# The causal triangle of an attention kernel: zeroed by GpSimd after the exponential, instead of added by matmuls before it

## The chip, the cores and the metric

The kernel runs on one core of a Trainium2 chip. The core has five engines that run their own instruction queues in order and meet through semaphores: TensorE (PE, matmuls into PSUM), VectorE (DVE), ScalarE (ACT), GpSimd (POOL) and SyncE (SP, which issues DMAs). The metric is the device time of one execution in microseconds; before the change it was 471.11 us, the median of three runs (469.35 to 471.49).

## The reference

Four blocks act on x, 2048 tokens by 512 channels in bfloat16: A, B, A, B, each added to its input. A is attention with 32 heads of 16 channels, in four segments of 512 tokens, causal within a segment, plus a memory that earlier segments fill. B is a linear attention with softmax features. The change touches A's causal mask above all.

```
# A, for each segment s
logits = einsum('bhqd,bhkd->bhqk', qs, ks) * scale + mask   # mask: -1e9 where key > query
p      = softmax(logits)
a_dot  = einsum('bhqk,bhkd->bhqd', p, vs)
pq, pk = phi(qs), phi(ks)                                   # phi(t) = t+1 if t > 0 else exp(t)
o      = g * (pq @ M) / (pq @ z + 1e-6) + (1 - g) * a_dot
M, z   = M + pk^T @ vs, z + sum(pk)
# then x = x + concat(o) @ wo;  before each block x is layer-normalised
```

## The kernel before

Tokens stand in 16 tiles of 128; a segment is four tiles. The whole of x stays in SBUF (`X`). For each tile `ln` takes mean and variance on DVE (L580, L581), the inverse root on GpSimd in two steps (L588 adds epsilon, L590 raises to the power -0.5), and the norm (x - mean) * rstd on DVE (L601). The result is transposed by a DMA, or by TensorE with `tpe` (L371) where `PE_T` names the tile.

`a_proj` makes keys and queries, transposed, for a segment. `kmask` (L642) copies the keys four times, each copy multiplied by a 0/1 column (`m4`) so that only one head of four is left (tile KM); `phi` (L632) makes the memory's features with an exponential on ACT and, on DVE, two clamps (L638, L639) and a sum (L640). All of these go from SBUF to SBUF.

`a_att` (L795) is called for two query tiles at a time (i0 = 0 and i0 = 2 of a segment). For each of the four head groups it makes score tiles S in PSUM with products that use 64 of TensorE's 128 rows each, two at a time side by side. There are three kinds of score tile: full ones below the diagonal (exponential into PT, 128 x 1024), two tiles of the query pair's own first key tile (`Sf`, exponential into PF, 896 columns) and one of the second key tile (`Sd`, into PE, 768 columns). Sf and Sd contain diagonal blocks of 64 x 64. On these, before the change, a further pair of products adds the triangle: the stationary `two64` (two identities side by side) times the moving `tri`, which holds -1e9 above the diagonal. ACT then takes the exponential of the whole tile, and the PV products use it with the values VT and their swapped copy VS (a DMA, "vsw").

```
# L828 (Sf) and L837 (Sd), the triangle's products at the end of each
(S.t[:, hf*512+64:hf*512+448].rearrange(...)[:, :, 0:64], two(hf), tri(hf, 2), False, True) for hf in range(2)
(S.t[:, hf*512:hf*512+384].rearrange(...)[:, :, 0:128],   two(hf), tri(hf, 4), False, True) for hf in range(2)
```

With 2 layers, 4 segments, 2 pairs of query tiles and 4 head groups there are 64 head-group passes, so 128 tiles PF and 64 tiles PE. PF lives in three buffers and PE in two (`N_PF`, `N_PE`); a buffer is opened by the score product and free again after the PV products. PSUM has four double tiles `D`, which score tiles, PV sums, projections and transposes share.

`out_proj` adds the output product to x; `b_keys` and `b_query` are block B. A few products use all 128 rows: the transposes of `tpe` (4 matmuls each), the sum of two halves in `o_T` (8 matmuls each, six times), the fold of B's feature weights in `fold_weights` (4 each, eight times), the product for the gates and the warm-up.

The order of the work is not decided in the code. `Graph.place` unpacks a table, `ORDER`: a position for every operation, the engine for each that may run on several, and a buffer for every tile. Each engine's queue follows these positions. `emit` then adds the semaphore waits that the data need; a wait is left out only between two operations of TensorE, so a GpSimd step that uses what an earlier GpSimd step wrote waits for it as well. Operations marked `port=True` are those that go from SBUF to SBUF.

Of the kernel before, what the change touches and what calls it, by code (L numbers as in the profile page):

```python
# [10 lines left out]
ALU = mybir.AluOpType  # L11
AX = mybir.AxisListType
BF16 = mybir.dt.bfloat16
F32 = mybir.dt.float32

S_TOK = 2048
D = 512
# [280 lines left out]
class Kernel:  # L298
# [72 lines left out]
    def tpe(self, out_ap, src, reads, writes, opens=(), label="", ev=None):  # L371

        ps = self.T(self.pD, "gen")
        pb = lambda: ps.t[:, :].bitcast(BF16)[:, 0:512]

        def fn(e):
            for k in range(4):
                ins = e.transpose(pb()[:, k * 128:(k + 1) * 128], src()[:, k * 128:(k + 1) * 128], self.ident[:])  # L378
            return ins
        self.g.op({"pe": (240.0, fn)}, list(reads) + [self.R("ident")], [ps], opens=opens, label=label + "p")  # L380
        if ev:
            self.evac(ev[0], lambda: ev[1](pb()), 512, [ps], writes, label=label + "e")
        else:
            self.evac(out_ap, lambda: pb().rearrange("p (a b) -> p a b", a=4), 512, [ps], writes, label=label + "e", fast=True)
# [11 lines left out]
    def alloc(self):  # L396
# [9 lines left out]
        self.two64 = sb("two64", [128, 2, 64], BF16)  # L406
# [43 lines left out]
    def setup(self):  # L450
# [43 lines left out]
        for g in range(NG):  # L494
            for hf in range(2):
# [16 lines left out]
        v(lambda e: e.tensor_tensor(self.two64[:], self.ident[:, 0:64][:, None, :].to_broadcast([128, 2, 64]),  # L512
                                    self.ident[:, 64:128][:, None, :].to_broadcast([128, 2, 64]), ALU.add), 120, [R("ident")], [R("two64")])
        tw = self.T(self.p1, "fold")
        v(lambda e: e.memset(tw.t[:, 0:128], -1e9), 150, [], [tw], eng=P)
        v(lambda e: e.affine_select(tw.t[:, 0:128], tw.t[:, 0:128], [[-1, 128]], ALU.is_gt, 0.0, base=0, channel_multiplier=1), 250, [tw], [tw], eng=P)
# [8 lines left out]
        self.mm(lambda: [(pb.t[:, 0:H], self.onesb[:], self.beta_sb[:], True, True)], [H], [R("beta0"), R("onesb")], [pb], label="beta")  # L525
# [22 lines left out]
    def fold_weights(self):  # L548
# [12 lines left out]
        for k in ("k", "q"):  # L561
# [7 lines left out]
            for dt in range(4):  # L569
                ps = self.T(self.pD, "gen")  # L570
                self.mm(lambda ps=ps, dt=dt, W=W: [(ps.t[:, g * 128:(g + 1) * 128], W.t[:, g, dt * 128:(dt + 1) * 128],
                                                    Wbd.t[:, g * 128:(g + 1) * 128], True, True) for g in range(NG)],
                        [128] * 4, [W[dt], Wbd], [ps], label="fold")
                self.evac(lambda k=k, dt=dt: self.WB[k][:, dt, :], lambda ps=ps: ps.t[:, 0:512], 512, [ps], [R("WB", k, dt)], label="folde")


    def ln(self, t, xT, flex=False, pe=False, root="pool"):
# [22 lines left out]
        else:  # L600
          v(lambda e: e.tensor_scalar(xn.t[:], self.X[:, t, :], self.mv[:, t, 0:1], self.rstd[:, t:t + 1],  # L601
                                    op0=ALU.subtract, op1=ALU.mult), 300,
          [R("X", t), R("mv", t), R("rstd", t)], [xn], label="xn", port=True)
# [28 lines left out]
    def phi(self, dst, src, e_, keys, c0, n):  # L632
# [5 lines left out]
        v(lambda e: e.tensor_scalar(cut(dst), cut(src), 0.0, None, op0=ALU.max), 68 + n / 3.84, S, D, label="phmax", port=True)  # L638
        v(lambda e: e.tensor_scalar(cut(e_), cut(e_), 1.0, None, op0=ALU.min), 68 + n / 3.84, E, E, label="phmin", port=True)  # L639
        v(lambda e: e.tensor_tensor(cut(dst), cut(dst), cut(e_), ALU.add), 68 + n / 1.92, D + E, D, label="phadd", port=True)  # L640

    def kmask(self, KM, KT, keys, c0, n, act):  # L642

        for sl in range(4):
            out = lambda sl=sl: KM.t[:, c0 // 128:(c0 + n) // 128, sl % 2, :, 64 * (sl // 2):64 * (sl // 2) + 64]
            src = lambda: KT.t[:, c0:c0 + n].rearrange("p (j h k) -> p j h k", h=2, k=64)
            ch = {"dve": (129 + n / 3.84, lambda e, sl=sl, out=out: e.tensor_scalar(out(), src(), self.m4[:, sl:sl + 1], None, op0=ALU.mult))}
            if act:
# [3 lines left out]
    def warm(self):  # L652
# [12 lines left out]
        for k in range(N_WARM):  # L665
            unit(128, 512, 1)
            if k == N_WARM // 2:
                for rows, n, m in ((64, 51, 12), (64, 64, 8), (64, 256, 4), (128, 34, 8)):
                    unit(rows, n, m)

    def a_proj(self, L, s):
# [66 lines left out]
        if s < 3:  # L738
            for hp in range(2):
# [10 lines left out]
                else:  # L750
# [3 lines left out]
                       [R("MS32", hp), R("GAm")], [R("MSb", s, hp)], label="Mmask")  # L754
# [523 lines left out]
```

## Time and profile before

| | |
|---|---|
| median of three runs | 471.11 us |
| span of the profiled execution | 465.9 us |
| instructions | 25071 |
| granted TensorE clock, mean | 0.999 |
| DVE instructions | 801 |
| GpSimd instructions | 139 |
| first to last triangle product, first layer | 16.5 to 181.3 us |
| first to last triangle product, second layer | 239.8 to 398.0 us |

The span runs from the first to the last instruction of the profiled execution and is shorter than the time of a run, which also has the start and the end of the program. Lines are named L and a number, as in the listing above. A busy share of TensorE counts overlapping matmuls once; a matmul's duration is longer than the interval to the next one, because they are pipelined. In rows of the trace "x4" means four instructions drawn together.

### The profile page before, as it was taken

To read this page: it belongs to the slowest core of one execution; us is meant where nothing else is said; L and a number is where in the kernel's file an instruction comes from. 1 tells how busy PE (TensorE), PEld (TensorE's weight loads), DVE (VectorE), ACT (ScalarE), POOL (GpSimd) and SP (SyncE) were. 2 spreads that over 40 slices of the span, in tenths; PEclk is the share of its full clock that TensorE was granted. 3 is DMA by queue.
4 is the path that set the end of the run, shared out by engine and by line. 5 is a ranking of instruction groups with operands and counts; after the bars stand their busy time and mean duration, and the time that the engine had idled before them with its cause. 6 is when DMAs were issued, how large, how long until landed. Compare 5 with 4: busy or idle time off the path is not lost.

```text
span 465.9 us, 25071 instructions
## 1 busy us (share of the span) xinstructions
PE 448.2 (96%) x11591; PEld 296.7 (64%) x11591; DVE 418.9 (90%) x801; ACT 424.3 (91%) x550; POOL 53.3 (11%) x139
## 2 busy tenths in 40 slices
PE   9999999999999999999999999999999999999886
PEld 4467656767767676655556777676677677666553
DVE  6999999999879988988999999999999787998991
ACT  4899999999999998589999999999999999686984
POOL 1401131001101101100320041010020020110000
PEclk9999999999999999999999999999999999999999
DMA  8363673403743031000143443441206104100247
GB/s 258 80 150 77 94 147 65 75 13 53 95 83 50 4 56 37 14 3 14 31 87 61 72 82 61 73 87 33 25 16 106 26 16 61 38 13 3 48 82 216
DMA packets 89386, 30.34 MB, mean 65 GB/s; under 512 B 75954, under 2 KB 89282, under 8 KB 89282
## 3 DMA queue, kind: packets, MB, share of 16 engines
q1 hardware_dynamic: 88450, 28.20, 32.5%
q8 instruction: 91, 1.49, 1.3%
q10 hardware_dynamic: 800, 0.52, 0.4%
q14 instruction: 13, 0.11, 0.1%
q0 software_dynamic: 32, 0.02, 0.0%
HBM read 6.31 MB, written 2.10 MB: 18 GB/s over the span
## 4 chain that ended last, share of the span: by engine, by line
PE 67%; ACT 26%; DVE 4%; issue 2%; POOL 1%; DVEq 0%
PE D L341 42%; PE D L326 23%; ACT p L351 12%; ACT pF L351 8%; ACT pE L351 4%; PE D L662 2%; DVE p L1091 1%; ACT pS L351 1%; PE D L378 1%; DVE p L360 1%; ACT X L359 1%; POOL rstd L590 1%; ACT p L359 0%; DVE p L601 0%; DVE p L1097 0%
## 5 line engine op out<-in xcount | busy, mean ns | idle before, releaser
L351 ACT ACTIVATE p<-D 128x1024 bf16<-128x1024 f32 (+1 forms) x224 | 222.0, 1026 | 13.2 <-PE D L341 10.0
L351 ACT ACTIVATE pF<-D 128x896 bf16<-128x896 f32 x128 | 116.1, 934 | 3.1 <-PE D L326 2.2
L326 PE MATMUL D<-pK,pQ 64*128 64x256 bf16 (+3 forms) x1536 | 114.8, 243 | 4.2 <-ACT pF L351 1.0
L326 PEld LDWEIGHTS D<-pK,pQ 64*128 64x128 bf16 x1536 | 55.1, 94 | 40.8 <-ACT pF L351 6.5
L326 PE MATMUL D<-pV,pF 64*128 64x34 bf16 x1024 | 76.4, 176 | 0.5 <-ACT pE L351 0.5
L326 PE MATMUL D<-pW,pF 64*128 64x34 bf16 x1024 | 74.1, 176 | 0.0
L326 PEld LDWEIGHTS D<-pV,pF 64*128 64x128 bf16 x1024 | 56.7, 93 | 3.7 <-issue 0.8
L588 POOL TENSOR_SCALAR rstd<-mv 128x1 f32<-128x1 f32 x60 | 15.2, 259 | 352.9 <-DVE mv L581 352.9
L326 PE MATMUL D<-pV,p 64*128 64x34 bf16 x1024 | 53.4, 176 | 0.6 <-issue 0.4
L326 PEld LDWEIGHTS D<-pW,pF 64*128 64x128 bf16 x1024 | 53.4, 93 | 1.0
L351 ACT ACTIVATE pE<-D 128x768 bf16<-128x768 f32 x64 | 52.4, 828 | 1.3 <-PE D L326 1.0
L326 PE MATMUL D<-pW,p 64*128 64x34 bf16 x1024 | 52.4, 176 | 0.0
L326 PEld LDWEIGHTS D<-pV,p 64*128 64x128 bf16 x1024 | 47.5, 93 | 3.2 <-issue 0.5
L326 PEld LDWEIGHTS D<-pW,p 64*128 64x128 bf16 x1024 | 46.0, 93 | 1.6
L326 PE MATMUL D<-tri,two 64*128 64x128 bf16 (+1 forms) x384 | 46.1, 234 | 0.0
L326 PE MATMUL D<-pV,pE 64*128 64x34 bf16 x512 | 45.1, 175 | 0.0
L580 DVE BATCH_NORM_STATS2 stats<-X 128x6 f32<-128x512 bf16 x64 | 42.7, 682 | 1.9 <-DMA X<-in_A_x_dram 1.5
L326 PE MATMUL D<-pW,pE 64*128 64x34 bf16 x512 | 43.4, 175 | 0.0
L972 DVE TENSOR_REDUCE pS<-p 128x64 f32<-128x1024 bf16 (+1 forms) x36 | 38.8, 1089 | 1.4 <-ACT p L351 1.4
L341 PE MATMUL D<-pX,WA_q 64*128 64x512 bf16 x256 | 37.1, 377 | 0.1
L341 PE MATMUL D<-pX,WA_k 64*128 64x512 bf16 x256 | 36.9, 377 | 0.1
L590 POOL TENSOR_TENSOR rstd<-rstd,mhalf 128x1 f32<-128x1 f32 x60 | 35.1, 599 | 3.1
(130 smaller groups left out, 986.2 us busy)
## 6 DMA issues: line engine op xcount, KB each, us to landing
pW<-pV SPq DMA_DIRECT2D x16, 136.0 KB, 3.1
out_dram<-X SPq DMA_DIRECT2D x7, 256.0 KB, 3.2
X<-in_A_x_dram SPq DMA_DIRECT2D x3, 512.0 KB, 5.6
pX<-in_B_wqkv_dram SPq DMA_DIRECT2D x3, 512.0 KB, 4.7
p<-p SPq DMA_TRANSPOSE x76, 3.0
pX<-p SPq DMA_TRANSPOSE x54, 3.3
WA_k<-in_A_wk_dram SPq DMA_DIRECT2D x2, 256.0 KB, 6.7
WB_o<-in_B_wo_dram SPq DMA_DIRECT2D x8, 64.0 KB, 3.0
```

What stands on the lines that cost most here:

```text
L326: ins = e.matmul(out_ap, lhsT, rhs, start=st, stop=sp, tile_position=(basep(lhsT), basep(out_ap)))
L341: ins = e.matmul(out_ap, lhsT[64 * hf:64 * hf + 64], rhs[64 * hf:64 * hf + 64], start=k == 0 and i == 0, stop=k == 1 and i == len(lists[hf ...
L351: return self.g.op({"act": (dur, lambda e: e.activation(out_ap(), in_ap(), func, scale=scale))}, reads, writes, opens, label=label)
L359: ch = {"act": (n / 1.2 + 51, lambda e: e.activation(out_ap(), in_ap(), ACT.Copy)), "dve": ((340 if fast else n / 0.96 + 65), lambda e: e. ...
L360: "dve": ((340 if fast else n / 0.96 + 65), lambda e: e.tensor_copy(out_ap(), in_ap()))}
L378: ins = e.transpose(pb()[:, k * 128:(k + 1) * 128], src()[:, k * 128:(k + 1) * 128], self.ident[:])
L580: v(lambda e: e.bn_stats(self.stats[:, t, :], self.X[:, t, :]), 602, [R("X", t)], [R("st", t)], label="bn")
L588: v(lambda e: e.tensor_scalar(rs, self.mv[:, t, 1:2], LN_EPS, None, op0=ALU.add), 170, [R("mv", t)], [R("rstd", t)], eng="pool", label="rstd")
L590: v(lambda e: e.tensor_tensor(rs, rs, self.mhalf[:], ALU.pow), 540, [R("rstd", t), R("mhalf")], [R("rstd", t)], eng="pool", label="rstd")
L662: ins = e.matmul(D.t[c0:, r0 * 8:r0 * 8 + n], r[:, c0:], ones(r, n), start=True, stop=True, tile_position=(r0, c0))
L972: fn = lambda e, sgn=sgn, eo=eo, Z=Z, n=n: e.tensor_reduce(Z.t[:, 0:64 * n].rearrange("p (k s h) -> p k s h", k=n, s=2)[:, :, sgn, :], eo( ...
L1091: v(lambda e, Ns=Ns, Tm=Tm, w=w, shape=shape: e.tensor_tensor(shape(Tm.t[:]), shape(Ns.t[:]), w(), ALU.mult), 600, [Ns, AB[0], AB[1]], [Tm ...
```

## The change

- The triangle's products are gone. The exponential of Sf and Sd now covers the diagonal blocks unmasked, and `causal` sets the entries of PF and PE above the diagonal to zero afterwards, on GpSimd: two steps for each tile, the first over all 128 rows (it clears the triangle of rows 64 to 127), the second over rows 0 to 63 (it clears theirs). Each step is two `affine_select` instructions, over 128 elements a row for PF and 256 for PE. The PV products wait for the second step. `CAUSAL_DVE`, which would do it on DVE, is empty.
- The products that used 128 rows use 64: each transpose becomes eight products of 64 rows against a 64 x 64 part of the identity, with float32 results in two PSUM banks instead of bfloat16 in one; the fold, the sum of halves, the gates and the warm-up likewise. The warm-up has one group less.
- The norm, the clamps of `phi` and the key masks may run on GpSimd.
- The order table is new. Unpacked, it gives GpSimd 22 of the 64 norms, 21 of the 72 masks and 11 of the 52 clamps (before: none), and the 384 steps of `causal`. Of the evictions and copies that DVE or ACT may do, ACT gets two of the four copies of `WB_v`'s permutation, one mask and one transpose eviction more, and one each fewer of four other kinds.
- Buffer counts and transfers stay as they were.

```diff
@@ tpe
-                ins = e.transpose(pb()[:, k * 128:(k + 1) * 128], src()[:, k * 128:(k + 1) * 128], self.ident[:])
+                for hf in range(2):
+                    r = slice(64 * hf, 64 * hf + 64)
+                    ins = e.matmul(ps.t[:, hf * 512 + k * 64:hf * 512 + k * 64 + 64], src()[r, k * 128:(k + 1) * 128], self.ident[r, r], start=True, stop=True,
+                                   tile_position=(64 * hf, 0))
...
@@ ln
-          v(lambda e: e.tensor_scalar(xn.t[:], self.X[:, t, :], self.mv[:, t, 0:1], self.rstd[:, t:t + 1],
-                                    op0=ALU.subtract, op1=ALU.mult), 300,
-          [R("X", t), R("mv", t), R("rstd", t)], [xn], label="xn", port=True)
+          norm = lambda e: e.tensor_scalar(xn.t[:], self.X[:, t, :], self.mv[:, t, 0:1], self.rstd[:, t:t + 1], op0=ALU.subtract, op1=ALU.mult)
+          ch = {"dve": (300, norm)}
+          if root != "act":
+              ch["pool"] = (610, norm)
+          self.g.op(ch, [R("X", t), R("mv", t), R("rstd", t)], [xn], label="xn", port=True)
@@ phi
-        v(lambda e: e.tensor_scalar(cut(dst), cut(src), 0.0, None, op0=ALU.max), 68 + n / 3.84, S, D, label="phmax", port=True)
-        v(lambda e: e.tensor_scalar(cut(e_), cut(e_), 1.0, None, op0=ALU.min), 68 + n / 3.84, E, E, label="phmin", port=True)
+        for fn, r, w, lab in ((lambda e: e.tensor_scalar(cut(dst), cut(src), 0.0, None, op0=ALU.max), S, D, "phmax"),
+                              (lambda e: e.tensor_scalar(cut(e_), cut(e_), 1.0, None, op0=ALU.min), E, E, "phmin")):
+            self.g.op({"dve": (68 + n / 3.84, fn), "pool": (170 + n * 0.86, fn)}, r, w, label=lab, port=True)
@@ kmask
+            ch["pool"] = (170 + n * 0.86, ch["dve"][1])
@@ new
+    def causal(self, P, blocks, n, label):
+
+        def sel(r, c0):
+            def fn(e):
+                for b in range(2):
+                    x = blocks(P.t[0:r], 64)[:, :, b, :]
+                    ins = e.affine_select(x, x, [[0, n], [1, 64]], ALU.is_ge, 0.0, base=c0, channel_multiplier=-1)
+                return ins
+            return fn
...
+            for r, c0 in ((128, 64), (64, 0)):
+                self.v(sel(r, c0), 2 * (187 + 0.43 * 64 * n), [P], [P], eng="pool", label=label)
@@ a_att, Sf
-                                for x in range(2) for hf in range(2)] + [
-                                (S.t[:, hf * 512 + 64:hf * 512 + 448].rearrange("p (b c) -> p b c", b=2)[:, :, 0:64], two(hf), tri(hf, 2), False, True) for hf in range(2)],
-                                [], rd + trir, [S], opens=[P], label="Sf", rows=64, dur=252)
+                                for x in range(2) for hf in range(2)],
+                                [], rd, [S], opens=[P], label="Sf", rows=64, dur=196)
...
+                            self.causal(P, lambda x, w: x[:, :, w:7 * w].rearrange("p a (b c) -> p a b c", b=2)[:, :, :, 0:w], 2, "Tf")
@@ a_att, Sd
-                    for p in range(2) for x in range(2) for hf in range(2)] + [
-                    (S.t[:, hf * 512:hf * 512 + 384].rearrange("p (a b) -> p a b", a=2)[:, :, 0:128], two(hf), tri(hf, 4), False, True) for hf in range(2)],
-                    [], rd + trir, [S], opens=[PE], label="Sd", rows=64, dur=286)
+                    for p in range(2) for x in range(2) for hf in range(2)],
+                    [], rd, [S], opens=[PE], label="Sd", rows=64, dur=177)
...
+                self.causal(PE, lambda x, w: x[:, :, w:3 * w].rearrange("p a (b c) -> p a b c", b=2), 4, "Td")
@@ order
+CAUSAL_DVE = set()
 ORDER = """
...
```

More of the change, by code (lines that the diff above doesn't have):

```diff
@@ L14 @@
 F32 = mybir.dt.float32
+I16 = mybir.dt.int16
+I32 = mybir.dt.int32
 S_TOK = 2048
@@ L893, in fn @@
                     for sgn in range(2):
-                        ins = e.matmul(tp.t[:, k * 128:(k + 1) * 128], pair.t[:, (k // 2) * 512 + sgn * 256 + (k % 2) * 128:(k // 2) * 512 + sgn * 256 + (k % 2) * 128 + 128],
-                                       self.ident[:], start=sgn == 0, stop=sgn == 1)
-                return ins
-            self.g.op({"pe": (440.0, fn)}, [pair, R("ident")], [tp], opens=[oT], label="otp")
-            self.evac(lambda: oT.t[:], lambda: tp.t[:, 0:512], 512, [tp], [oT], label="ote")
+                        for hf in range(2):
+                            r = slice(64 * hf, 64 * hf + 64)
+                            c0 = (k // 2) * 512 + sgn * 256 + (k % 2) * 128
+                            ins = e.matmul(tp.t[:, hf * 512 + k * 64:hf * 512 + k * 64 + 64], pair.t[r, c0:c0 + 128], self.ident[r, r], start=sgn == 0, stop=sgn == 1,
+                                           tile_position=(64 * hf, 0))
+                return ins
+            self.g.op({"pe": (220.0, fn)}, [pair, R("ident")], [tp], opens=[oT], label="otp", rows=64)
+            self.evac(lambda: oT.t[:].rearrange("p (a h c) -> p h a c", a=4, h=2),
+                      lambda: tp.t[:].rearrange("p (h x) -> p h x", h=2)[:, :, 0:256].rearrange("p h (a c) -> p h a c", a=4), 512, [tp], [oT], label="ote")
         elif key in PE_T:
```

169 lines of the change are left out of this document (88 added, 81 removed).

## The prediction

> **What bounds the kernel now.** I read the page's shares first, then the chain of waits, then busy time by stage, then the groups by line.
>
> ```profile
> PE 448.2 (96%) x11591; PEld 296.7 (64%) x11591; DVE 418.9 (90%) x801; ACT 424.3 (91%) x550; POOL 53.3 (11%) x139
> PE 67%; ACT 26%; DVE 4%; issue 2%; POOL 1%; DVEq 0%
> 16.50:181.30 164.80, 160.79 (x4534) 110.53 (x4532) 153.22 (x287) 159.89 (x195) 18.90 (x44) 1.00 0.42 73
> 239.80:398.00 158.20, 154.97 (x4557) 109.20 (x4553) 144.96 (x260) 156.38 (x190) 17.48 (x44) 1.00 0.33 56
> 0.00:16.50 16.50, 15.14 (x153) 7.11 (x155) 11.88 (x38) 8.53 (x20) 5.51 (x26) 1.00 0.66 196
> 181.30:239.80 58.50, 56.62 (x1168) 34.02 (x1166) 53.56 (x116) 49.62 (x73) 8.13 (x19) 1.00 0.13 25
> 398.00:466.00 68.00, 60.68 (x1201) 35.82 (x1196) 55.25 (x104) 49.91 (x77) 3.25 (x8) 0.99 0.29 68
> ```
>
> The last five rows cut the span where the first and the last triangle product of each layer stand (columns: length, PE, PEld, DVE, ACT, POOL busy). In the two attention stages (323 us) ACT is 97% and 99% busy with exponentials, PE 98%; outside them PE leads and ACT idles. The granted clock is 1.00, so no term below is a clock's. The chain gives PE 67% because PE and ACT release each other in turn. Three engines are full and GpSimd (POOL) is empty: that is the room the change uses.
>
> **What it removes from PE.** The triangle products are 384 matmuls.
>
> ```profile
> L326 PE MATMUL D<-tri,two 64*128 64x128 bf16 x256 | 28.5, 215 | 0.0
> L326 PE MATMUL D<-tri,two 64*128 64x256 bf16 x128 | 17.6, 270 | 0.0
> 45.87 0.22 PE L326 MATMUL D<-tri,two 64*128 64x128 bf16 x2
> 45.92 0.18 PE L326 MATMUL D<-pV,pF 64*128 64x34 bf16 x1
> 46.59 0.27 PE L326 MATMUL D<-tri,two 64*128 64x256 bf16 x2
> 46.70 0.18 PE L326 MATMUL D<-pV,pF 64*128 64x34 bf16 x1
> 38.33 0.22 PE L326 MATMUL D<-tri,two 64*128 64x128 bf16 x2
> 38.48 0.40 PE L378 MATMUL D<-ident,p 128*128 128x128 bf16 x4
> 38.81 0.19 PE L326 MATMUL D<-pV,p 64*128 64x34 bf16 x1
> ```
>
> Matmuls overlap, so I price them by start to next start: a pair of 128 columns costs 0.05 us, a pair of 256 columns 0.11. 128 x 0.05 + 64 x 0.11 = 13.4 us, all of it in the attention stages. A 128-row transpose of four (last three rows) takes 0.05 from the triangle pair's start, then 0.43 until the next 64-row product starts. As eight 64-row products of 64 columns it is four pairs of about 0.03 (the 128-column pair, halved), 0.11 in all: 0.32 saved. The 24 such groups (16 transposes, 8 folds) save 8 us, the six pair sums some 2 more. PE loses 23 of its 448 us.
>
> In the attention stages that is worth little by itself: ACT leaves 164.8 - 159.9 = 4.9 and 158.2 - 156.4 = 1.8 us, so the 13.4 can give 6.7 at most there, unless the new order pulls projections in. Outside them PE leads, and about half of the groups (5 us) lie there; with the norms that leave DVE I take 6 us off. The order table of the diff, unpacked (a place and an engine for each operation), hands ACT no less work: some ten evictions move between ACT and DVE, about even. ACT's 424 us stay.
>
> **What it adds to GpSimd.** 128 tiles PF and 64 tiles PE get two steps of two selections each: 512 over 128 elements, 256 over 256.
>
> ```profile
> 1.18 0.28 POOL L510 TENSOR_SCALAR_AFFINE_SELECT ident<-ident 128x128 bf16<-128x128 bf16 x1
> 1.43 0.09 POOL L501 MEMSET mhalf<- 128x1 f32 x1
> 1.88 0.19 POOL L503 TENSOR_SCALAR_AFFINE_SELECT H<-ones 128x8 f32<-128x8 f32 x1
> 2.14 0.19 POOL L505 TENSOR_SCALAR_AFFINE_SELECT H<-H 128x8 f32<-128x8 f32 x1
> 14.47 0.56 POOL L542 MEMSET pE<- 128x256 bf16 x2
> L588 POOL TENSOR_SCALAR rstd<-mv 128x1 f32<-128x1 f32 x60 | 15.2, 259 | 352.9 <-DVE mv L581 352.9
> L590 POOL TENSOR_TENSOR rstd<-rstd,mhalf 128x1 f32<-128x1 f32 x60 | 35.1, 599 | 3.1
> ```
>
> A selection over 128 elements runs 0.28 us, and an independent next instruction starts 0.25 after it. One that waits for the first (the two H rows) starts 2.14 - 2.07 = 0.07 after its end; the second step of a tile waits for the first step in this way. A PF tile holds GpSimd for 4 x 0.25 = 1.0 us if another tile's step stands between, 1.1 if not; I take 1.05. The 256-element selection is not in the trace: from below it costs a start interval of 0.25 (the two 256-element memsets, 0.56 for both at 0.31 each), from above 0.19 + 248 x (0.28 - 0.19)/120 = 0.38. So a PE tile takes 1.0 to 1.53 us; I take the middle, 1.27. Each layer has 64 and 32 tiles: 67 + 41 = 108 us (96 to 119).
>
> The order also leaves two power steps for each norm (0.26 + 0.60): 39 and 46 steps fall between a layer's first and last selection, 17 and 19 us. And it gives GpSimd 22 norms, 21 key masks and 11 clamps. The slope of the memsets (0.11 us for 128 elements more than 0.20) on the 0.22 of a one-element step prices a 512-element one at 0.65, a 1024-element one at 1.08; between the selections stand 6 norms, 9 masks, 6 clamps (some of 512) in the first layer, 7, 7 and 4 in the second: 16 us each. GpSimd's own demand is **141 us** of the first stage and **143** of the second, against ACT's 160 and 156. It fits, with a tenth to spare, if nothing delays it.
>
> **What delays it.** GpSimd and DVE keep each other from SBUF:
>
> ```profile
> L601 DVE TENSOR_SCALAR p<-X,mv,rstd x64: 314/407/985, 7.0 to 410.6; 128x512 bf16<-128x512 bf16 x64
> 14.33 1.30 DVE L601 TENSOR_SCALAR p<-X,mv,rstd 128x512 bf16<-128x512 bf16 x2
> 14.97 0.20 POOL L544 MEMSET pF<- 128x128 bf16 x1
> 17.33 0.48 POOL L544 MEMSET pF<- 128x128 bf16 x1
> L588 POOL TENSOR_SCALAR rstd<-mv x60: 203/221/567, 12.4 to 409.1; 128x1 f32<-128x1 f32 x60
> 105.88 0.61 POOL L590 TENSOR_TENSOR rstd<-rstd,mhalf 128x1 f32<-128x1 f32 x1
> 105.98 0.47 DVE L647 TENSOR_SCALAR pQ<-p,m 128x1024 bf16<-128x1024 bf16 x1
> L647 DVE TENSOR_SCALAR pQ<-p,m 128x1024 bf16<-128x1024 bf16 (+1 forms) x71 | 30.4, 447 | 0.4 <-ACT p L359 0.3
> L640 DVE TENSOR_TENSOR p<-p 128x1024 bf16<-128x1024 bf16 (+1 forms) x26 | 16.5, 641 | 0.1
> ```
>
> The norm that takes 407 ns as a rule took 985 when it met the three memsets from 14.47 on; a memset of 0.20 took 0.48 beside another norm; the one-element step goes from 221 to 567. But at 105.88 a mask starts inside a power step and is not slowed, nor the step by much (0.61 against 0.60): the exclusion is partial. Between the first and the last selection the order leaves DVE 95 and 103 operations from SBUF to SBUF (masks, norms, clamps, sums, adds); at 0.41 to 0.64 each these are 43 and 47 us. If half of that time is taken from GpSimd, its stages need 141 + 21.5 = 162.5 and 143 + 23.5 = 166.5 us, and DVE, relieved of 9 us a stage, gets them back as waits. The bounds are no collision and full exclusion (184 and 190).
>
> The Trainium skill, page "SBUF — State Buffer", section "SBUF: two separate sides", calls this pair an exclusive lock held for the whole instruction, the other engine blocked fully. By that the sum would be the full exclusion; the trace agrees for the norm (985) and not for the mask inside the power step.
>
> Nor is the demand even. In a layer's steps with i0 = 0 a head group needs on ACT:
>
> ```profile
> L351 ACT ACTIVATE pF<-D 128x896 bf16<-128x896 f32 x128 | 116.1, 934 | 3.1 <-PE D L326 2.2
> L351 ACT ACTIVATE pE<-D 128x768 bf16<-128x768 f32 x64 | 52.4, 828 | 1.3 <-PE D L326 1.0
> ```
>
> 2 x 0.93 + 0.83 = 2.70 us, on GpSimd 2 x 1.05 + 1.27 = 3.37. With three PF and two PE buffers, unchanged, GpSimd cannot run far behind: a late selection holds its PV products on PE, these hold the buffer, and the next score product, which opens the buffer, leaves ACT idle; PE's queue is in order, so projections behind the PV products wait too. On GpSimd, power steps stand behind a selection that waits for its exponential, and behind them a norm, its transposing DMA and a projection. 32 such groups x 0.67 = 21 us; ACT's other work in these stretches (evictions, key exponentials) covers more than half, and I add 8 us.
>
> DMA is left as it is: no transfer is added, and the one on POOL's queue stands at the start of both orders. The evictions of the 64-row transposes read float32 instead of bf16; DVE's 11.6 us of slack in the first stage covers the few. The new latency (1 to 1.5 us between exponential and PV) costs nothing beyond the above while other tiles' work stands between; where it does not, PE waits.
>
> **The sum,** against the execution's own 465.9: first stage 162.5 - 164.8 = -2.3; second 166.5 - 158.2 = +8.3; unevenness +8; outside -6. That is +8, span 474. The median of the runs, 471.1, is 5.2 above the span: **480 us**, two per cent slower.
>
> **Rivals.**
> *GpSimd keeps up: faster.* If collisions cost GpSimd under 13 us a stage, or the 256-element selection costs nearer 0.25, its need stays below ACT's 156, the stages shrink to ACT's pace (-4.9 - 1.8), outside -6: span 453, run 458; with the other 6.7 us of the triangle's PE time filled by projections from outside, 452. For it: of a 128-element selection's 0.28 us the slope gives 0.09 to the elements, and if only that part shuts DVE out, few operations meet; against it: the 985. The deciding point is GpSimd's need passing ACT's 156 us, 13 us above its own demand in the second stage.
> *Full exclusion: much slower.* 184 and 190 us give +19 + 32 + 8 - 6 = +53, run 524; with the low price of selections (129 + 43 and 131 + 47) and no unevenness it is +7 + 20 - 6, run 492. The 985 and 567 speak for it, the 0.47 mask against.
> *Nothing moves.* ACT's 97 to 99% hides the triangle's 13.4 us, and GpSimd's delays use up the 12: 471.
>
> **The numbers.** A change under 0.5% (2.4 us) can't be told from none here. Forecast (474 to 492) 0.44, full exclusion (above 492) 0.14, nothing 0.08, GpSimd keeps up 0.34. So slower 0.58, same 0.08, faster 0.34. The range runs from the fast rival's 452 to 508, inside the strict one; the forecast's own is 474 to 492.
>
> **What would show it.** Right: tri rows gone and PE's busy time near 425; POOL some 290 to 330 busy and over 85% in the stages; selections' mean above 0.30 at 128 elements; DVE's norms and masks longer than 407 and 447; PE waiting for POOL in the list of waits, ACT idle in the stages. Wrong: POOL with gaps in the stages, its wait rows naming ACT, and ACT still at 97%; then the fast rival holds.

## The result, and the profile after

The changed kernel takes **580.15 us** (median of four runs, 576.85 to 583.71) against 470.94 for the kernel before on the same chip: a ratio of 1.234, 95% interval 1.228 to 1.240. The forecast was 480 with a range to 508. The direction was right, the size was not: 110 us slower, not 9. In what follows a time is the median of all executions of a kernel, while a ratio leaves out executions more than 1.5% above the fastest of the same kernel, which matters in one place.

From the page of the kernel after: busy times, the granted clock in 40 slices, and the chain of waits by engine and by line.

```profile
PE 472.6 (81%) x11369; PEld 293.8 (51%) x11369; DVE 436.0 (75%) x747; ACT 433.1 (74%) x550; POOL 426.5 (73%) x960
PEclk9987898878989979999889989988798987999999
POOL 49%; PE 28%; DVE 9%; ACT 8%; issue 3%; DMA 3%; POOLq 0%; SPq 0%; DVEq 0%
PE D L343 17%; POOL pF L769 16%; POOL pE L769 11%; PE D L328 9%; POOL pQ L653 8%; POOL p L604 5%; ACT p L353 4%; POOL rstd L593 3%; DMA p<-p 3%; ACT pF L353 3%; POOL p L644 2%; POOL p L643 1%; PE D L669 1%; POOL rstd L591 1%; DVE p L1117 1%
```

GpSimd went from 53.3 to 426.5 us busy and leads the chain with 49%. Line numbers have moved: L769 are the selections, L604 the norm, L653 the mask, L643 and L644 the clamps, L328 the 64-row products, L343 the projections, L353 the exponentials.

The same by stage, from the first to the last exponential of a diagonal tile in each layer, then the rest (columns: length, busy PE, PEld, DVE, ACT, POOL, granted clock, DMA share, GB/s):

```profile
18.00:234.00 216.00, 168.88 (x4288) 105.68 (x4286) 157.97 (x253) 163.24 (x194) 195.41 (x444) 0.89 0.27 51
301.40:510.00 208.60, 168.51 (x4306) 106.65 (x4304) 155.66 (x247) 162.40 (x190) 189.63 (x445) 0.90 0.26 45
0.00:18.00 18.00, 15.80 (x209) 7.62 (x211) 13.23 (x39) 9.85 (x21) 10.33 (x29) 1.00 0.87 235
234.00:301.40 67.40, 59.08 (x1287) 36.66 (x1280) 53.10 (x110) 48.78 (x71) 18.48 (x29) 0.92 0.11 19
510.00:582.00 72.00, 60.35 (x1302) 37.22 (x1298) 56.05 (x103) 48.89 (x76) 12.63 (x17) 0.99 0.31 63
120.00:140.00 20.00, 16.05 (x348) 8.78 (x342) 13.15 (x19) 14.93 (x17) 19.04 (x35) 0.92 0.19 39
```

Between the same marks (18.1 to 181.6 and 240.0 to 398.6) the stages took 163.5 and 158.6 us before; they now take 216 and 208.6. GpSimd is busy 195 and 190 us of them, where the prediction gave it 141 and 143 of its own; in the 20 us of the last row it is busy 19. ACT, at 97 to 99% before, is at 76 and 78%. What fills GpSimd stands in its groups (shape, count, busy us, mean ns, idle before):

```profile
L769 POOL TENSOR_SCALAR_AFFINE_SELECT pF<-pF 128x128 bf16<-128x128 bf16 x256 | 78.3, 330 | 23.7 <-ACT pF L353 23.6
L769 POOL TENSOR_SCALAR_AFFINE_SELECT pF<-pF 64x128 bf16<-64x128 bf16 x256 | 76.6, 322 | 3.1
L769 POOL TENSOR_SCALAR_AFFINE_SELECT pE<-pE 64x256 bf16<-64x256 bf16 x128 | 54.1, 444 | 1.3
L769 POOL TENSOR_SCALAR_AFFINE_SELECT pE<-pE 128x256 bf16<-128x256 bf16 x128 | 51.9, 427 | 10.1 <-ACT pE L353 9.9
L604 POOL TENSOR_SCALAR p<-X,mv,rstd 128x512 bf16<-128x512 bf16 x22 | 46.5, 2113 | 1.0
L653 POOL TENSOR_SCALAR pQ<-p,m 128x1024 bf16<-128x1024 bf16 x14 | 40.8, 2916 | 7.1 <-ACT p L361 7.1
L644 POOL TENSOR_SCALAR p<-p 128x1024 bf16<-128x1024 bf16 x5 | 13.9, 2786 | 0.4
L653 POOL TENSOR_SCALAR pQ<-p,m 128x512 bf16<-128x512 bf16 x7 | 11.4, 1633 | 0.4 <-ACT p L361 0.4
L643 POOL TENSOR_SCALAR p<-p 128x1024 bf16<-128x1024 bf16 x2 | 5.5, 2770 | 0.0
```

The selections are a little over their forecast: 0.32 to 0.33 us against 0.28, and 0.43 to 0.44 against 0.38 as the upper end. The moved operations are far over theirs: a norm takes 2.11 us where 0.65 was forecast, a mask or clamp of 1024 elements 2.8 to 2.9 where 1.08 was. The 50 of the 54 in these rows hold GpSimd for 118 us; at the forecast's prices they would hold it for 22 x 0.65 + 21 x 1.08 + 7 x 0.65 = 42. Within the two stages the moved operations take 56 and 46 us by the sum of their durations in the trace, where the prediction had 16 each.

Who waits, some rows from the list of waits of the kernel after (engine, tile and line; releaser; us, times, longest):

```profile
ACT pF L353 <- PE D L328: 52.6, 41, 4.9
PE D L328 <- POOL pF L769: 36.9, 30, 5.1
PEld D L328 <- POOL pF L769: 35.4, 38, 4.4
DVE pS L394 <- PE D L328: 34.3, 22, 4.3
PEld D L328 <- POOL pE L769: 27.1, 24, 3.7
POOL pF L769 <- ACT pF L353: 23.6, 21, 3.5
PE D L328 <- POOL pE L769: 20.8, 20, 3.6
```

PV products wait for selections, and ACT for score products that stand behind them in PE's queue. A stretch of GpSimd's timeline in the first layer shows why a selection is late (start, us, what):

```profile
125.28 2.79 POOL L644 TENSOR_SCALAR p<-p 128x1024 bf16<-128x1024 bf16 x1
128.04 0.56 POOL L593 TENSOR_TENSOR rstd<-rstd,mhalf 128x1 f32<-128x1 f32 x1
128.60 2.10 POOL L604 TENSOR_SCALAR p<-X,mv,rstd 128x512 bf16<-128x512 bf16 x1
130.66 1.70 POOL L769 TENSOR_SCALAR_AFFINE_SELECT pF<-pF 128x128 bf16<-128x128 bf16 x4
132.36 4.13 POOL L604 TENSOR_SCALAR p<-X,mv,rstd 128x512 bf16<-128x512 bf16 x2
136.45 0.54 POOL L769 TENSOR_SCALAR_AFFINE_SELECT pF<-pF 128x128 bf16<-128x128 bf16 x2
```

Of 11.7 us, one clamp, one power step and three norms take 9.6, and the selections queued behind them stand still. PE's longest wait for a selection, at another place, is 5.1 us.

### The profile page after: what moved, and what is told of

It is laid out like the page before. It is cut to its first block, busy times and chain, and to the rows that moved or that the text cites. A ratio compares the mean times of both kernels' runs of the same rounds, so it can differ in the third digit from the quotient of the medians.

```text
span 581.7 us, 25426 instructions
## 1 busy us (share of the span) xinstructions
PE 472.6 (81%) x11369; PEld 293.8 (51%) x11369; DVE 436.0 (75%) x747; ACT 433.1 (74%) x550; POOL 426.5 (73%) x960
## 4 chain that ended last, share of the span: by engine, by line
POOL 49%; PE 28%; DVE 9%; ACT 8%; issue 3%; DMA 3%; POOLq 0%; SPq 0%; DVEq 0%
PE D L343 17%; POOL pF L769 16%; POOL pE L769 11%; PE D L328 9%; POOL pQ L653 8%; POOL p L604 5%; ACT p L353 4%; POOL rstd L593 3%; DMA p<-p 3%; ACT pF L353 3%; POOL p L644 2%; POOL p L643 1%; PE D L669 1%; POOL rstd L591 1%; DVE p L1117 1%
## 5 line engine op out<-in xcount | busy, mean ns | idle before, releaser
L353 ACT ACTIVATE p<-D 128x1024 bf16<-128x1024 f32 (+1 forms) x224 | 221.0, 1014 | 48.1 <-PE D L328 26.6
L769 POOL TENSOR_SCALAR_AFFINE_SELECT pF<-pF 64x128 bf16<-64x128 bf16 (+1 forms) x512 | 153.3, 326 | 26.8 <-ACT pF L353 23.6
L353 ACT ACTIVATE pF<-D 128x896 bf16<-128x896 f32 x128 | 116.4, 921 | 53.7 <-PE D L328 52.6
L328 PE MATMUL D<-pK,pQ 64*128 64x256 bf16 (+3 forms) x1536 | 122.0, 262 | 13.6 <-ACT pF L353 2.8
L769 POOL TENSOR_SCALAR_AFFINE_SELECT pE<-pE 64x256 bf16<-64x256 bf16 (+1 forms) x256 | 105.9, 436 | 11.4 <-ACT pE L353 9.9
L328 PE MATMUL D<-pV,pF 64*128 64x34 bf16 x1024 | 82.2, 181 | 36.8 <-POOL pF L769 22.4
L328 PEld LDWEIGHTS D<-pV,pF 64*128 64x128 bf16 x1024 | 59.6, 97 | 47.8 <-POOL pF L769 19.0
L328 PEld LDWEIGHTS D<-pK,pQ 64*128 64x128 bf16 x1536 | 57.1, 99 | 52.8 <-ACT pF L353 9.9
L328 PE MATMUL D<-pW,pF 64*128 64x34 bf16 x1024 | 79.6, 181 | 0.7 <-issue 0.7
L328 PE MATMUL D<-pV,p 64*128 64x34 bf16 x1024 | 55.6, 181 | 26.3 <-POOL pF L769 14.5
L328 PEld LDWEIGHTS D<-pV,p 64*128 64x128 bf16 x1024 | 48.6, 97 | 37.7 <-POOL pF L769 16.3
L353 ACT ACTIVATE pE<-D 128x768 bf16<-128x768 f32 x64 | 51.9, 815 | 14.6 <-PE D L328 13.8
L653 POOL TENSOR_SCALAR pQ<-p,m 128x1024 bf16<-128x1024 bf16 (+1 forms) x21 | 52.3, 2488 | 7.5 <-ACT p L361 7.5
L328 PEld LDWEIGHTS D<-pW,pF 64*128 64x128 bf16 x1024 | 55.7, 97 | 1.7 <-issue 0.8
L328 PE MATMUL D<-pW,p 64*128 64x34 bf16 x1024 | 54.7, 181 | 0.8 <-issue 0.8
L328 PEld LDWEIGHTS D<-pW,p 64*128 64x128 bf16 x1024 | 47.0, 97 | 3.0 <-issue 1.1
L604 POOL TENSOR_SCALAR p<-X,mv,rstd 128x512 bf16<-128x512 bf16 x22 | 46.5, 2113 | 1.0
L328 PE MATMUL D<-pV,pE 64*128 64x34 bf16 x512 | 47.1, 180 | 0.0
L328 PE MATMUL D<-pW,pE 64*128 64x34 bf16 x512 | 45.2, 180 | 0.0
L343 PE MATMUL D<-WB_k,pX 64*128 64x512 bf16 (+1 forms) x288 | 39.0, 393 | 4.1 <-issue 3.9
```

The costliest lines, as they stand in the source:

```text
L328: ins = e.matmul(out_ap, lhsT, rhs, start=st, stop=sp, tile_position=(basep(lhsT), basep(out_ap)))
L343: ins = e.matmul(out_ap, lhsT[64 * hf:64 * hf + 64], rhs[64 * hf:64 * hf + 64], start=k == 0 and i == 0, stop=k == 1 and i == len(lists[hf ...
L353: return self.g.op({"act": (dur, lambda e: e.activation(out_ap(), in_ap(), func, scale=scale))}, reads, writes, opens, label=label)
L604: norm = lambda e: e.tensor_scalar(xn.t[:], self.X[:, t, :], self.mv[:, t, 0:1], self.rstd[:, t:t + 1], op0=ALU.subtract, op1=ALU.mult)
L769: ins = e.affine_select(x, x, [[0, n], [1, 64]], ALU.is_ge, 0.0, base=c0, channel_multiplier=-1)
```

## The experiments

The theory: the price of the moved operations makes GpSimd late, and everything else follows. The rivals: GpSimd and DVE shut each other out of SBUF; the selections' second step puts a wait on each PV product; the new order costs by itself. "New order" below means the table of the kernel after, "old order" that of before. Ratios are to the kernel before on the same chip (469 to 470 us each time), with the 95% interval.

### The moved operations

First all 54 go back to DVE, at the places they have in the new order; then the norms alone stay on GpSimd, or the masks and clamps alone; then all 54 go to GpSimd in the kernel before.

```diff
 # e1: engine in the order table, 22 norms, 21 masks, 11 clamps
-pool
+dve
 # e2: the same for masks and clamps only;  e2b: for norms only
 # e3: before.py, old order, ln, phi and kmask of the kernel after, the same 54 operations
-dve
+pool
```

> The changed kernel with the 22 norms, 21 masks and 11 clamps back on DVE at their places in the same order; the selections stay on GpSimd. Price theory: these 54 instructions took 125 us of GpSimd (2.1 us a norm, 2.9 a mask, 2.8 a clamp) where the prediction had about 48, and every selection behind them waited; without them GpSimd needs some 310 us and the time falls from 580 to 475 to 500, with the clock back above 0.97. Selection theory (the selections, their latency and the shared access with DVE cost the time): little comes back, over 540. Clock theory (the lower clock, 0.914, is a cause of its own): the clock stays near 0.91.

> The changed kernel with the masks and clamps back on DVE; the 22 norms (2.1 us each, 46 us) and the selections stay on GpSimd. Price theory, by GpSimd time: the norms hold 46 of the 125 us that the moved instructions took, 37% of the 57 us between 523 and 580: 535 to 555.

> The changed kernel with the norms back on DVE; 21 masks and 11 clamps (79 us of GpSimd) and the selections stay. Price theory, by GpSimd time: 63% of the 57 us: 550 to 570.

> The kernel before, in its own order, with only the same 54 instructions given to GpSimd; triangle products and 128-row products stay. Price theory: GpSimd is free otherwise (53 us + 125 us), so each instruction is late by its own price only; those in front of scores (masks) and of a projection (norms) delay PE: 480 to 510. Selection theory: within 1% of before, 466 to 476, since GpSimd is free.

Measured: all back on DVE 523.05 (1.113, 1.110 to 1.117); norms alone on GpSimd 530.05 (1.126, 1.121 to 1.131); masks and clamps alone 559.97 (1.193, 1.188 to 1.198); all 54 in the kernel before 505.43 (1.077, 1.073 to 1.080). So the move costs 0.121 of 470 = 57 us in the kernel after. That is half of the 110, and the first run misses both of its forecasts (475 to 500 if the price were all, over 540 if the selections were): the price theory holds for half of the loss, and the other half is something else. The move's parts are 7 and 37 us alone, less than both together, and the norms cost less than their 46 of the 125 us would give; a reading that fits is that each further microsecond on GpSimd costs more the longer its queue is already. Even in the kernel before, where GpSimd is otherwise all but empty, the move costs 36 us.

Is it their own price, or SBUF held by DVE? Durations of the norms on GpSimd in the kernel after (min/median/max ns, first and last start):

```profile
L604 POOL TENSOR_SCALAR p<-X,mv,rstd x22: 2062/2094/2578, 17.9 to 525.0; 128x512 bf16<-128x512 bf16 x22
```

In the kernel before with the same 54 operations on GpSimd:

```profile
L601 POOL TENSOR_SCALAR p<-X,mv,rstd 128x512 bf16<-128x512 bf16 x22 | 47.1, 2142 | 1.1
L650 POOL TENSOR_SCALAR pQ<-p,m 128x1024 bf16<-128x1024 bf16 x14 | 42.5, 3034 | 44.9 <-DVE p L360 23.1 <-ACT p L359 21.8
```

The shortest norm of 22 takes 2.06 us, and the price is the same in two orders with different neighbours. It is the operation's own.

### The selections, and the exclusion from SBUF

From the kernel with the 54 operations back on DVE (523.05) one thing is changed at a time: each step of two selections becomes one that holds GpSimd about as long but touches one element or two; the second step is left out; DVE does the triangle with one minimum; the triangle's products come back in place of the selections.

```diff
 # e9
-ins = e.affine_select(x, x, ...)            # twice a step
+ins = e.tensor_tensor(self.scr[:, c:c + 1], self.ones8[:, 0:1], self.mhalf[:], ALU.pow)
+if n == 4:
+    ins = e.tensor_scalar(self.scr[:, c + 1:c + 2], self.ones8[:, 0:1], 1.0, None, op0=ALU.add)
 # e12
-for r, c0 in ((128, 64), (64, 0)):
+for r, c0 in ((128, 64),):
 # e7
-CAUSAL_DVE = set()
+CAUSAL_DVE = {"Tf", "Td"}
 # e6: a_att, two64 and tri of before.py, new order without the steps of causal
```

> As e1_moves_back (norms, masks and clamps on DVE), but each step's two selections are replaced by one-element GpSimd work of about the same time that leaves PF and PE alone: a power (0.56 us) for PF, a power and an addition for PE; the waits between exponential, GpSimd and PV stay. The triangle is then not masked. Exclusion theory (GpSimd and DVE keep each other from SBUF: in e1 a selection took 334 and 446 ns on average where the undisturbed ones take 288 and 409): the time falls from 523 to 500 or less. Waiting theory (what costs is that PV waits for two steps in a row behind each exponential): 512 to 530.

> As e1_moves_back, without the second step of each tile (rows 0 to 63 stay unmasked): GpSimd's selections fall from 268 to about 134 us and the time from exponential to PV by half. Waiting theory: more than half of the 53 us over before comes back, 480 to 497. If only the new order or the 64-row products were to blame: 515 or more.

> As e1_moves_back, with the triangle applied by DVE instead (one minimum against a triangle tile for each PF and PE, 192 instructions at the place of the first step). Each costs 0.25 to 0.45 us, some 60 us more on an engine that is busy 437 of 526 us. Waiting theory: the step from exponential to PV is one instruction of under half a microsecond but queues behind DVE's other work: 495 to 530. Exclusion theory: no GpSimd work beside DVE's, below 500.

> The new order and the 64-row products, with the triangle products back in the score products, no selection at all, and norms, masks and clamps on DVE. Waiting theory: the order itself is harmless, 465 to 485. Order theory (the new order is worse by itself): 500 or more.

Measured: 522.4 (1.113, 1.106 to 1.120); 508.92 (1.072, 1.067 to 1.077); 550.21 (1.170, 1.167 to 1.174); 500.94 (1.066, 1.064 to 1.069). With products for selections 22 us are gone (1.113 to 1.066): the selections cost 22 us where the prediction saw room for them on GpSimd and some gain on PE.

The groups of one-element steps in the run that has them, then two of the four groups of selections that they replace, in the kernel with the 54 operations on DVE (the other two take 79.0 and 55.2 us):

```profile
L772 POOL TENSOR_TENSOR scr<-ones,mhalf 128x1 bf16<-128x1 f32 x384 | 231.1, 616 | 70.4 <-ACT pF L353 48.9 <-ACT pE L353 15.4
L774 POOL TENSOR_SCALAR scr<-ones 128x1 bf16<-128x1 f32 x128 | 34.8, 272 | 2.3
```

```profile
L769 POOL TENSOR_SCALAR_AFFINE_SELECT pF<-pF 128x128 bf16<-128x128 bf16 x256 | 79.8, 334 | 51.9 <-ACT pF L353 51.6
L769 POOL TENSOR_SCALAR_AFFINE_SELECT pE<-pE 128x256 bf16<-128x256 bf16 x128 | 53.5, 440 | 20.6 <-ACT pE L353 20.4
```

The norms on DVE, with the selections and then with the one-element steps (min/median/max ns, first and last start):

```profile
L604 DVE TENSOR_SCALAR p<-X,mv,rstd x64: 374/407/1147, 7.1 to 469.1; 128x512 bf16<-128x512 bf16 x64
L605 DVE TENSOR_SCALAR p<-X,mv,rstd x64: 316/408/496, 6.9 to 464.7; 128x512 bf16<-128x512 bf16 x64
```

The steps hold GpSimd for 266 us against 268 for the selections and read and write next to nothing. DVE is then undisturbed (no norm over 0.50 us, against 1.15; 15 us less busy, 422.8 against 437.4), and the time is the same, 522.4 and 523.05: **the delay that the selections put on DVE costs nothing.** The delay that DVE puts on the selections is not tested by this. A selection over 128 elements takes 334 and 331 ns in the mean against a median of 287 in the same run, over 256 elements 440 and 452 against 408; that makes some 33 us of the 268, an estimate, and the steps were as long as the stretched selections. What is shown is that GpSimd's occupied time and the wait behind it cost 22 us, with or without shared rows in SBUF.

Without the second step the selections' time on GpSimd is halved (134 us), and each PV product waits for one step instead of two. By the ratios 19 us of the 22 are gained (14 by the medians; the four executions spread from 501.84 to 513.68), so half of the selections cost far less than half. The time, 504 by the ratio, lies between the two forecasts (480 to 497, or 515 and more). Whether the wait or the occupied time counts more was not separated. On DVE the triangle costs 27 us more than on GpSimd, above what either theory expected.

### The new order

In the old order, the selections stand right behind the exponential (products elsewhere as before); and the kernel before, unchanged in its code, runs in the new order, with the moved operations on DVE.

```diff
 # e4: before.py, a_att and causal of the kernel after, old order, each tile's two steps right behind its exponential
 # e13: before.py
-ORDER = (old order)
+ORDER = (new order without the steps of causal, the 54 operations on dve)
```

> The kernel before, in its own order, with the triangle products replaced by the selections on GpSimd, each right behind its exponential in the order; nothing else moved, 128-row products stay. Price theory: selections alone are bearable: 470 to 500. Selection theory: over 530. If the old order leaves no room between exponential and PV, the added 1.2 to 1.8 us for each tile shows as PE waiting for POOL.

> The kernel before, triangle products and 128-row products included, in the new order, with norms, masks and clamps on DVE. If the new order itself is what costs in e6 (501): 490 to 505. If it was the 64-row products in the new order: 465 to 480.

Measured: 604.68 (1.288, 1.283 to 1.292), far above the 470 to 500 of the price theory and as its rival had it (over 530), and 508.88 (1.081, 1.076 to 1.087). Rows from the list of waits with the selections in the old order:

```profile
POOL pF L762 <- ACT pF L351: 105.2, 60, 6.1
DVE p L601 <- POOL rstd L590: 52.0, 17, 6.6
PEld D L326 <- POOL pF L762: 49.6, 42, 4.1
ACT p L351 <- PE D L326: 41.7, 46, 5.6
```

GpSimd waits for exponentials, PE for GpSimd and ACT for PE in turn: the old order has the PV products close behind the exponential, with no room for the step between. So with selections the new order is much the better (523 against 605; other places for them in the old order were not tried). But it costs 38 us of its own, with not one instruction of the code changed. "Order" stands here for all that the table sets: compared with the table of the kernel before, it also gives 15 of the 2729 operations another engine (7 from DVE to ACT, 7 back, one from GpSimd to DVE) and 1128 of the 1493 tiles another buffer. Where the 38 us arise, the chain of waits of that run shows in one place (start, us, what), and so does the row of PE's waits that has grown most (5.5 in the kernel before):

```profile
216.17 0.72 DVE KV L938
216.89 0.34 DVE p L601
217.23 0.02 issue
217.25 4.40 DMA pX<-p
221.65 0.05 issue
221.69 0.39 PE D L341 x3
```

```profile
PEld D L341 <- issue: 27.5, 46, 3.1
```

A norm ends on DVE, its transposing transfer is issued 0.02 us later and takes 4.4, and the projection waits for it. (The list names a releaser only near the wait's end; these transfers land under "issue".) In the kernel before, no transfer stands in the chain. Of the time in which PE neither multiplies nor loads weights (gaps of more than 0.05 us, some 39 us in all), 18 us end with such a transfer, 11 of them behind a norm; in the kernel before it is about 1 of 12. So these gaps grow by some 27 us; PE is also busy 13 us longer (460.8 against 448.2). To see whether the wait for such a transfer is a cost or only a name for one, the transfers behind a norm read X instead of the norm, in both orders:

```diff
-            self.tr(dst, lambda: xn.t[:], [xn], [xT[tt]], label="xnT")
+            self.tr(dst, lambda: self.X[:, t, :], [R("X", t)], [xT[tt]], label="xnT")
```

> The kernel before in the new order, but the transfers that transpose a norm's result read X instead, so they no longer wait for the norm; the norms still run, nothing reads those that were transposed by DMA, and the result is that of attention on unnormalised rows. In the profile of the new order with the old code, PE's gaps of over 0.05 us sum to 38 us against 12 in the kernel before; 18 of them end with a transposing transfer that had been issued as its input got ready and landed 4 us later, 10.6 of these behind a norm. Theory (the new order puts these norms too close to their projections): 494 to 502, 7 to 15 us under the 508.9 of the new order alone. Rival (each such wait only hides another one, the order costs elsewhere): 505 to 511.

> The same edit in the kernel before, as the control: transfers that transpose a norm's result read X, so the result is that of unnormalised rows. PE's waits for such transfers sum to 0.2 us there. Both theories: 466 to 472.

Measured: 495.24 (1.059, 1.051 to 1.067) in the new order, 469.99 (1.002, 1.000 to 1.004) in the old. The new order's cost falls by 11 us (by the ratios) to 14 (by the medians); the control does not move. The same row after the edit:

```profile
PEld D L341 <- issue: 11.6, 18, 1.9
```

So about a third of the order's 38 us is norms that come too close before their projections. The other 24 to 27 lie in PE's waits for DVE, ACT and the transposed outputs of attention and in its longer busy time, and were not taken apart further.

### The 64-row products

The prediction took 23 us of PE's time off, 10 of them for the 64-row products, and 6 off the sum for what lies outside the stages. All of the 64-row edits in the old order, all but the transposes, and then three of them alone:

```diff
 # e5: before.py, old order, with tpe, warm, o_T, fold_weights and the gates' product of the kernel after
 # e14: the same without tpe
 # e17: fold_weights alone
 # e18: the pair sums of o_T alone
 # e19: the warm-up alone
```

> The kernel before, in its own order, with only the 128-row products turned into 64-row ones (transposes, fold, sum of halves, gates, warm-up). The prediction's term: 5 to 8 us less, 463 to 467. Clock theory: the 64-row warm-up or products bring the granted clock down: below 0.97 and slower than before.

> As e5 (64-row products in the old order, 476.5), but the transposes stay 128-row products with bfloat16 results; fold, sum of halves, gates and warm-up use 64 rows. If the transposes' float32 results and their longer evictions cost the 6.6 us of e5: 466 to 471. If the other 64-row products cost it: 474 to 478.

> The kernel before, old order, only the eight weight folds as 64-row products (64 matmuls of 64 columns in place of 32 of 128, with their evictions reading two halves). Prediction's term: 8 x 0.32 = 2.6 us less PE, 468 to 471. Rival from the run with all 64-row edits but the transposes (480.5): if the folds are what costs there, 474 to 481.

> The kernel before, old order, only the pair sums of the attention output as 64-row products. Prediction's term: 2 us less PE, 469 to 471. Rival: if these sums are what costs in the run with all 64-row edits but the transposes (480.5), 474 to 481.

> The kernel before, old order, only the warm-up products ahead of the first work at 64 rows instead of 128, one shape fewer. Prediction: nothing, 470 to 472. Rival: if a colder start of the matrix engine is what costs in the run with all 64-row edits but the transposes (480.5), 474 to 481, with a lower granted clock at the start.

Measured: 476.53 (1.015, 1.011 to 1.020), 480.52 (1.022, 1.017 to 1.027), folds 476.76 (1.013, 1.010 to 1.017), pair sums 472.0 (1.005, 1.003 to 1.007), warm-up 471.92 (1.005, 1.002 to 1.007). All are slower, by 0.5 to 2.2%; of the three alone, the folds most. Without the 64-row transposes the rest is no faster than with them, so the transposes are not the cause. In the new order it is the other way: from 508.88 with the old code to 500.94 with 64-row products.

The folds themselves are shorter, near the forecast's saving of 0.32: in the four groups with no wait of PE at either end and the same narrow matmul ahead, the start of the matmul ahead and the start of the one behind are 0.44 to 0.53 us apart with 128 rows and 0.12 to 0.22 with 64, 0.30 to 0.32 less (the evictions take 0.68 in both). The loss is elsewhere. Waits of PE's matmuls for nothing that the profile names, in the run with the folds alone and then in the kernel before:

```profile
PE D L326 <- issue: 7.4, 11, 1.3
PE D L341 <- issue: 1.5, 4, 0.8
```

```profile
PE D L326 <- issue: 0.9, 2, 0.4
PE D L341 <- issue: 0.3, 1, 0.3
```

8.9 us in 15 waits against 1.2 in three: the difference of 7.7 is about the folds' 7 us. The longer ones with the folds, and the first two before, have no semaphore ahead of them; the last section comes back to them. What shifts them from one kernel to the other was not settled.

## Why the prediction was right or wrong

The direction was right, and so was the engine: GpSimd becomes the bound, PE waits for it, ACT idles. The 110 us come, in one order of undoing, as 38 for the order (508.88), 8 back for 64-row products (500.94), 22 for selections (523.05) and 57 for the moved operations (580.15). The signs named for the forecast are mostly there: no rows of tri, GpSimd 90% busy in the stages, PE waiting for it and ACT idle; GpSimd's 426 us are far over the 290 to 330.

**The step that failed** is the price of the moved operations: "The slope of the memsets (0.11 us for 128 elements more than 0.20) on the 0.22 of a one-element step prices a 512-element one at 0.65, a 1024-element one at 1.08 [...] 16 us each". They measure 2.11 and 2.8 to 2.9 us, and in place of 16 us a stage they hold GpSimd for 56 and 46. A memset only writes; nothing in the profile before showed GpSimd reading a wide bfloat16 row and writing it through an arithmetic operation. This term had one price and no upper end, unlike the selections beside it (96 to 119 us). GpSimd is busy 54 and 47 us more in the stages than the 141 and 143 of the sum; 40 and 30 of these are the moved operations. Undoing the move gives back 57 of the 110 us; the 57 is the cost of the whole move and not of the mispricing alone. The entries that the diff gives the planner of the order (610 ns for a norm, 170 + 0.86 n for the others, so 1.05 us at 1024) are as low. The Trainium skill, page "GPSIMD Engine Reference", section "4.1 Engine selection", calls GpSimd's elementwise work with one input roughly line-rate; the trace does not agree: a 1024-element mask takes 2.92 us there and 0.47 on DVE in the kernel before.

**The order** had no term at all. The prediction looked at what the table hands to each engine and found ACT's share even; it did not ask whether the old work runs as well in the new sequence. It named the chain ("behind them a norm, its transposing DMA and a projection") only as a part of the 8 us for unevenness. The order alone costs 38 us, 11 to 14 of them by that chain; why it costs the rest stays open.

**The selections** were priced nearly right one by one, and were 45 us of GpSimd's time over the sum's figure (261 against 216), some 26 of them, an estimate, by the stretch that the prediction counts separately (next paragraph). The sentence that the latency between exponential and PV "costs nothing beyond the above while other tiles' work stands between" held in neither order: 22 us in the new one, where the triangle's products were taken away in exchange, and 135 in the old one, both with the time on GpSimd in them.

**The exclusion** from SBUF was given 45 us of GpSimd's time in the sum. The stretch is there: selections at 330 ns, above the 0.30 that was named as its sign, and DVE's norms and masks longer than the 407 and 447 of before, by the groups of the kernel after (the mask's row mixes two widths):

```profile
L653 DVE TENSOR_SCALAR pQ<-p,m 128x1024 bf16<-128x1024 bf16 (+1 forms) x49 | 29.2, 606 | 1.5 <-ACT p L361 1.5
L604 DVE TENSOR_SCALAR p<-X,mv,rstd 128x512 bf16<-128x512 bf16 x42 | 20.2, 491 | 7.6 <-POOL rstd L593 7.6
```

In GpSimd's time it is smaller than forecast: the selections' means of 330 and 322 ns against a median of 288, and of 444 and 427 against 409, make some 26 us, an estimate. Its other side, the time that DVE loses, has no price in the run with one-element steps. What GpSimd's own stretch costs was not separated, since those steps were as long as the stretched selections. The rival of full exclusion (492 to 524) comes nearest to the time, but by luck: what makes GpSimd late is above all the price of the moved operations.

**PE's 23 us**: the 64-row products are worth 8 us in the new order and cost 7 in the old. That the 8 lie close to the 6 taken is partly luck, since the 6 also counted the norms that leave DVE, and the same edits lose time in the old order. "PE's busy time near 425" is far off (472.6): the granted clock is 0.91, and the matmuls are longer (a score product of 256 columns takes 289 ns against 270). The clock was no term of the sum. It is 0.91 here, where PE is busy 81% of the span; 0.96 and 87% with the moves undone; 0.98 and 90% without selections as well; 1.00 and 96% in the kernel before: the clock rises with PE's busy share. Which of the two drives the other, and how much of the 110 us the lower clock adds, no run separates.

## What to carry to other kernels

An operation that the trace of an engine does not show has no price there: before moving work to a lightly used engine, run one instance of that very operation at that width, or carry an upper end for it into the sum. A new order of the same work is a change of its own, to be run alone with the old code. When two engines disturb each other visibly, replace one's work by something that occupies it as long without the disturbance, and see whether the time moves; if it does not, the other engine's delay was free, and the replaced engine's own delay is still to be tested.

## What the runs showed of the hardware

- On GpSimd, a one-operation step on bfloat16 takes 1.63 us for 512 and 2.92 for 1024 elements a row, so 2.5 ns an element; the norm, with two operations and two column operands, 2.06 for 512. A selection's median is 288 ns for 128 elements and 409 for 256, 0.95 ns an element.
- PE stalls without a semaphore, at places in its instruction stream that recur from kernel to kernel. Counted in matmuls, the stalls of over 0.2 us with the folds changed stand ahead of numbers 1872, 2765, 3277, 3659, 4297, 4425, 4808 and further; with the warm-up changed ahead of 1872, 2765, 3277, 3659 and 6587; in the kernel before there are two, 1237 and 1872. The steps between them, up to 4808, are 1, 3, 4, 5 or 7 times about 128 matmuls, with their weight loads 256 instructions. The page of the run with the folds has a queue that moves instructions, in 91 pieces of 16 KB (columns: packets, MB, share):

```profile
q8 instruction: 91, 1.49, 1.3%
```

  The Trainium skill, page "Runtime: NRT & Kernel Launch", section "Instruction fetch mechanics", says that an engine's instructions are refilled in blocks of 16 KiB, 256 instructions, at a cost that is mostly hidden. The steps agree with the block. If the stalls are such refills, the cost is not hidden here: single ones reach 1.3 us, and PE's unnamed waits make 8.9 us in the run with the folds. That the fetch is late there was not tested.
